# First feed-forward product in pairs of units: 64-row products of two units on the two halves of the array's rows

## The chip, the cores and the metric

The kernel runs on one core of a Trainium2 chip. The metric is the device time of one execution in microseconds. Before the change the median of three runs is 411.9 us (411.26 to 412.43).

## What is computed

The input x has 2048 rows (tokens) of 448 values. With xn the layer norm of x, the output is x, plus a spectral filter of xn, plus a mixer of xn:

```
X = rfft2(xn) * (w_r + 1j * w_i);  A = irfft2(X)              # 2048 x 448
h = gelu(layernorm(xn) @ w1);  hs = shift(h) @ w2;  x1 = xn + hs
B = x1 + gelu(layernorm(x1) @ w3) @ w4                         # w3: 448 x 1792, w4: 1792 x 448
out = x + A + B
```

The change concerns `layernorm(x1) @ w3`, the first product of the feed-forward part.

## The kernel before, in words

All products run in f16 and carry each operand as a high and a low part; a product is the sum of three passes, high by high, high by low and low by high. The 448 rows of w3 are a contraction of three full strips of 128 and a last strip of 64. `w3p` holds high parts in strips 0 to 3 and low parts in strips 4 to 7; strip 3 holds its 64 rows twice, in the lower and the upper half of the partitions, and so does strip 7. The tokens' side `x2all` holds strips 0 to 3 high and 4 to 6 low; in strip 3 the partitions 0 to 63 are the high part of the last 64 values and partitions 64 to 127 their low part. So strip 3 of `w3p` by strip 3 of `x2all` is two passes in one product, and strip 7 by strip 3 is the third pass (`mlp_in`, L425 to L429, the product itself at L427). That makes 3 + 3 + 3 + 2 = 11 products for each block of 128 columns of w3.

The feed-forward work is cut into 56 units: 8 groups G of 256 tokens by 7 pieces fp of 256 columns. `front` (L745) makes a unit's 22 products of 128x256 into one PSUM bank (L427), then ScalarE applies gelu in place (L753) and writes the high part (L756), and VectorE writes the low part (L757) to a tile `hf`, of which there are three. `back` (L761) multiplies `hf` by w4 (L776), 12 products of 448 columns, into the group's two accumulators. `mlp` (L791) calls these in turn: for groups 0 to 2 two units ahead, alternately on the banks tagged "mm" and "tr" (two of each), from group 3 on one unit ahead, on the two "mm" banks.

A scheduler with priorities and a model of time orders the instructions of each engine; the feed-forward work has the lowest priority (FILL), so it fills TensorE between the steps of the other branch. Those are step1 (L594), and then 16 chunks, each with products at L651 (pp), L668 (px) and L697 (pu) and conversions on ScalarE, VectorE and GpSimd (L658 to L701), and at the end the inverse transform (L717, L739). Between the 56 units stand also w_scale_end (L617, L621), which spreads one scale: L621 multiplies a single row. Other products that a step below uses are L254 (a sum over partitions, one column), L406 (the turning of x by an identity, of 128 and of 64 columns) and L456 and L501 (w1 and w2).

`ln2` (L512) writes each block of 128 tokens as `h`, 896 columns: 0 to 447 high, 448 to 511 the low part of the last 64, 512 to 895 the other low parts. SyncE turns it with a DMA transpose into `x2all` (L544). The other transposes on SyncE's queue are those of the w1 result (L483, `h<-hs`) and of x (L833).

Of the kernel before, what the change touches and what calls it, by code (L numbers as in the profile page):

```python
# [13 lines left out]
F16 = mybir.dt.float16  # L14
# [17 lines left out]
AH = 2  # L32
# [89 lines left out]
def body(tc, nc, x, wf, w1, w2, w3, w4, c_g, c_n, c_small, out):  # L122
    V, A, P, T, SY = nc.vector, nc.scalar, nc.gpsimd, nc.tensor, nc.sync
# [28 lines left out]
    def bank(tag, name):  # L152
        return ps.tile([128, 512], F32, tag=tag, bufs=2, name=name)
# [3 lines left out]
    pw = pool("pw")  # L157
# [62 lines left out]
    load_x(3)  # L220
    load_w3([2, 3])
    x2mem = pw.tile([128, 9 * F], F16, name="x2mem")
    x2all = x2mem[:, 0:8 * F].rearrange("p (j t n) -> p j t n", j=4, t=7)
    w4raw = x2mem.bitcast(F32)[:, F:].rearrange("p (f n) -> p f n", f=14)
    W4F = (0, 4, 8, 11, 14)
# [198 lines left out]
    def mlp_in(ps_out, wp, cols, xT, tok, ts=range(4)):  # L424
        for t in ts:  # L425
            for wi, xi in ((0, 0), (0, 4), (4, 0)) if t < 3 else ((0, 0), (4, 0)):
                T.matmul(ps_out, wp[:, wi + t, cols], xT[:, xi + t, tok],  # L427
                         start=t == 0 and wi + xi == 0, stop=t == 3 and wi == 4)


    w3p = pa.tile([128, 8, F], F16, name="w3p")
# [79 lines left out]
    def ln2(bs, engines, pins=None):  # L511

        n, b0 = len(bs), bs[0]
        mv = stats([xb(b) for b in bs], f"b{b0}")
        a = pc.tile([128, 4], F32, tag="vb", bufs=2, name=f"vb{b0}")[:, :n]
        r = pc.tile([128, 4], F32, tag="vs", bufs=2, name=f"vs{b0}")[:, :n]
        o, y = [], []
        nm = pc.tile([128, 4], F32, tag="nm", bufs=2, name=f"nm{b0}")[:, :n]
        P.tensor_scalar(out=nm, in0=mv[:, :n, 0], scalar1=-1.0, scalar2=None, op0=ALU.mult)
        for m in range(0, n, 2):  # L520
            w = stage(f"y{b0 + m}", 8 * 448, 0 if pins else (b0 + m) // 2 % 2, F16)
            o.append(w[:, 0:4 * D].bitcast(F32).rearrange("p (i n) -> p i n", i=2))
# [12 lines left out]
        for i in range(n):  # L535
            b, h, x_ = b0 + i, y[i // 2][:, i % 2], o[i // 2][:, i % 2]
            k = r[:, i:i + 1]
            with behind("f", *pins[i]) if pins else contextlib.nullcontext():
                u = A.activation(out=h[:, 0:D], in_=x_, func=AF.Copy, scale=k)
                V.scalar_tensor_tensor(out=h[:, 448:512], in0=x_[:, 384:448], scalar=k, in1=h[:, 384:448],  # L540
                                       op0=ALU.mult, op1=ALU.subtract)
                v = V.scalar_tensor_tensor(out=h[:, 512:896], in0=x_[:, 0:384], scalar=k, in1=h[:, 0:384],
                                           op0=ALU.mult, op1=ALU.subtract)
            d = SY.dma_start_transpose(out=x2all[:, b // 4][:, :, 128 * (b % 4):128 * (b % 4) + 128], in_=h)  # L544
            after[f"b{b0}"] = u.ins, v.ins, d.ins

    def unscaled(b, t=None):
# [194 lines left out]

    acc, hs, rest = {}, {}, {}

    def front(G, fp, tag):  # L745
        tok = slice(256 * (G % 2), 256 * (G % 2) + 256)
        pm = bank(tag, f"pw3_{G}{fp}")
        for ff in range(2):
            f = 2 * fp + ff
            mlp_in(pm[:, 256 * ff:256 * ff + 256], w3p, slice(128 * f, 128 * f + 128), x2all[:, G // 2], tok)  # L750
        with prio(EVAC):
            with behind("te", 12) if (G, fp) == (4, 1) else contextlib.nullcontext():
                A.activation(out=pm, in_=pm, func=AF.Gelu_apprx_tanh, scale=r3)  # L753
            h = pw.tile([128, 2, 512], F16, tag="hf", bufs=3, name=f"hf{G}{fp}")
            with behind("te", 10 + 2 * fp) if (G, fp) in ((4, 1), (4, 2)) else contextlib.nullcontext():
                i = A.activation(out=h[:, 0], in_=pm, func=AF.Copy, scale=h3)  # L756
                j = V.scalar_tensor_tensor(out=h[:, 1], in0=pm, scalar=h3, in1=h[:, 0], op0=ALU.mult, op1=ALU.subtract)  # L757
            after["f", G, fp] = i.ins, j.ins
        hs[G, fp] = h
# [28 lines left out]
                    V.scalar_tensor_tensor(out=xb(b), in0=acc[G][i][:, :D], scalar=p34[:, 0:1], in1=xb(b),  # L788
                                           op0=ALU.mult, op1=ALU.add)

    def mlp(Gs, last=False, hook=None, ahead=1, tags=("mm",)):  # L791
        with prio(FILL):
            todo = [(G, fp) for G in Gs for fp in range(7)]
            done = 0
            for n, (G, fp) in enumerate(todo):
                while done < min(n + 1 + ahead, len(todo)):
                    front(*todo[done], tags[done % len(tags)])
                    if hook:
                        with prio(EVAC):
                            hook(*todo[done])  # L800
                    done += 1
                if fp == 3 and last:
                    for b in (2 * G, 2 * G + 1):
                        rest[b] = unscaled(b, x2mem.bitcast(F32)[:, D * (b - 12):D * (b - 11)])
                back(G, fp)


    wps = bank("mm", "wps")
# [136 lines left out]
    for k in range(4):  # L945
        n = 128 if k < 3 else 64
# [39 lines left out]
        w4_split(2)  # L986

    def w4_rest(G, fp):
        if fp < 5:
# [21 lines left out]
    mlp([1, 2], ahead=AH, tags=("mm", "tr"))  # L1011
    for b in range(0, NB, 2):
        do_fold(b)
        step1_in(b)
# [22 lines left out]
        if 0 <= i - 3 < NC:  # L1037
            chunk_c(i - 3)
    close("pst")
    mlp(range(3, 6))  # L1040
    pv = pool("pv", side="right")
    bs = [*range(12, 16), *range(8, 12), *range(8)]
    units = [(G, fp) for G in range(4, 8) for fp in range(7)][INV:]
# [9 lines left out]
                finish(bs[n])  # L1053

    inverse(range(4))
    mlp([6], last=True)
    inverse(range(4, 16))
    mlp([7], last=True)
    for name in ("pv", "pa2", "pa", "pw", "px", "pc", "ps"):
        close(name)  # L1060

# [23 lines left out]
```

## Time and profile before

| | |
|---|---|
| median of 3 runs | 411.9 us |
| span of the profiled execution | 409.9 us |
| its own time: the span, and some 2.0 us around it by the median | about 411.9 us |
| granted TensorE clock | 1.000 |
| instructions | 8512 |
| TensorE weight loads (PEld) busy | 288.1 us |
| VectorE busy | 294.8 us |
| ScalarE busy | 247.8 us |
| GpSimd busy | 116.8 us |
| mean DMA traffic | 121 GB/s |

Busy time of TensorE is from the starts of its products to modelled ends, which overlap; what a product costs in a row of products is the distance from start to start. In the listings a row of the timeline is start, length, engine, line, operation, tiles, shapes and count, neighbours of one line merged; a row of the chain is start, length, engine, tile, line and count.

### The profile page before, as it was taken

Reading aid. Unit: us, or ns where it says so; the run is one execution under the profiler, and the core shown is the slowest. Engines: PE = TensorE matmul, PEld = TensorE weight load, DVE = VectorE, ACT = ScalarE, POOL = GpSimd, SP = SyncE. Lnnn points to the kernel's source line nnn. Section 1 sums busy time; section 2 is a strip of 40 time slices with the busy share of each in tenths; the row PEclk is TensorE's granted clock in tenths of the full one; section 3 lists DMA queues with packets and bytes.
Section 4 is the critical chain, followed back from the end, with each engine's and each line's share of the span. In section 5 each row is a group of like instructions: output and inputs, shape, how many; then the busy total and the mean of one; then the engine's idle time right before and its main releaser. Section 6 shows DMA issues by size and latency. Waiting matters only on the chain.

```text
span 409.9 us, 8512 instructions
## 1 busy us (share of the span) xinstructions
PE 404.8 (99%) x3295; PEld 288.1 (70%) x3295; DVE 294.8 (72%) x642; ACT 247.8 (60%) x427; POOL 116.8 (29%) x206
## 2 busy tenths in 40 slices
PE   8999999999999999999999999999999999999996
PEld 4554556666677877776887887877776777677885
DVE  5989999898644658863689889875777787667122
ACT  4689994884738756861688888873343434342321
POOL 3889820002308745400021221111222221121000
PEclk9999999999999999999999999999999999999999
DMA  8999999907712283527056555610000213223001
GB/s 278 335 269 200 172 178 248 269 2 183 137 43 56 79 300 106 143 63 164 14 162 167 145 147 142 182 43 2 2 0 2 73 55 100 91 76 128 24 0 46
DMA packets 57208, 49.45 MB, mean 121 GB/s; under 512 B 41312, under 2 KB 52192, under 8 KB 57168
## 3 DMA queue, kind: packets, MB, share of 16 engines
q1 hardware_dynamic: 57168, 48.91, 45.5%
q8 instruction: 26, 0.43, 0.4%
q14 instruction: 14, 0.11, 0.1%
HBM read 35.06 MB, written 3.67 MB: 95 GB/s over the span
## 4 chain that ended last, share of the span: by engine, by line
PE 96%; DMA 1%; POOL 1%; DVE 1%; issue 0%; POOLq 0%
PE pw L427 33%; PE acc L776 31%; PE pw L501 9%; PE pw L456 6%; PE pu L697 3%; PE ps L594 3%; PE pp L651 2%; PE pe L717 2%; PE px L668 2%; PE py L739 2%; PE wps L812 2%; DMA h<-hs 1%; PE pta L406 1%; POOL w2s L273 0%; POOL w2s L901 0%
## 5 line engine op out<-in xcount | busy, mean ns | idle before, releaser
L427 PE MATMUL pw<-x2mem,w3p 128*128 128x256 f16 x1232 | 149.1, 272 | 0.0
L776 PE MATMUL acc<-w4p,hf 128*128 128x448 f16 (+1 forms) x714 | 138.0, 341 | 0.0
L427 PEld LDWEIGHTS <-w3p 128*128 128x128 f16 x1232 | 118.6, 98 | 19.0
L776 PEld LDWEIGHTS <-hf 128*128 128x128 f16 x714 | 69.4, 98 | 48.3 <-DVE hf L757 0.3
L753 ACT ACTIVATE pw<-pw,pe 128x512 f32<-128x512 f32 x56 | 36.7, 655 | 63.1 <-PE pw L427 62.0
L757 DVE SCALAR_TENSOR_TENSOR hf<-pw,h,hf 128x512 f16<-128x512 f32 x56 | 42.0, 749 | 44.7 <-ACT hf L756 44.3
L756 ACT ACTIVATE hf<-pw,h 128x512 f16<-128x512 f32 x56 | 38.3, 684 | 1.2
L501 PE MATMUL pw<-w2p,h 112*128 112x448 f16 x192 | 38.8, 352 | 0.1
L678 POOL TENSOR_TENSOR z<-te 128x450 f32<-128x450 f32 x16 | 16.0, 1001 | 72.9 <-DVE te L676 69.1
L456 PE MATMUL pw<-w1p,xT 128*128 128x448 f16 x176 | 34.9, 352 | 0.5 <-DVE h L875 0.5
L724 POOL TENSOR_TENSOR e<-e 128x226 f32<-128x226 f32 x16 | 11.5, 720 | 77.8 <-ACT e L721 74.6
L501 PEld LDWEIGHTS <-h 112*128 112x128 f16 x192 | 18.5, 98 | 16.9 <-DMA h<-hs 0.9
L456 PEld LDWEIGHTS <-xT 128*128 128x128 f16 x176 | 17.0, 98 | 16.4 <-ACT xT L416 0.7
L658 ACT ACTIVATE pf<-pp 64x450 f16<-64x450 f32 x32 | 17.3, 541 | 16.7 <-DVE pf L659 8.3
L721 ACT ACTIVATE e<-pe 128x452 f32<-128x452 f32 x16 | 8.8, 547 | 26.4 <-PE pe L717 26.4
L659 DVE TENSOR_TENSOR pf<-pp,pf 64x450 f16<-64x450 f32 x32 | 19.9, 621 | 5.8 <-ACT pf L658 5.6
L574 POOL TENSOR_TENSOR xr<-xf 128x452 f32<-128x452 f32 x8 | 8.9, 1109 | 35.9 <-issue 27.1
L673 ACT ACTIVATE te<-px 64x450 f32<-64x450 f32 x32 | 17.2, 537 | 0.5
L585 DVE TENSOR_TENSOR xh<-f,xh 128x452 f16<-128x452 f32 x16 | 13.4, 878 | 5.3 <-ACT xh L584 5.3
L732 DVE TENSOR_TENSOR vh<-e,vh 128x448 f16<-128x448 f32 x16 | 10.0, 624 | 9.7 <-ACT vh L731 9.7
L577 POOL TENSOR_TENSOR f<-xr 128x452 f32<-128x452 f32 x16 | 16.4, 1045 | 0.6
L726 DVE TENSOR_TENSOR e<-e 128x113 f32<-128x113 f32 x16 | 9.9, 619 | 7.8 <-POOL e L724 7.8
(171 smaller groups left out, 598.8 us busy)
## 6 DMA issues: line engine op xcount, KB each, us to landing
wc<-wf SPq DMA_DIRECT2D x32, 225.0 KB, 3.5
wl<-wf SPq DMA_DIRECT2D x8, 450.0 KB, 4.1
xf<-x SPq DMA_DIRECT2D x8, 448.0 KB, 3.5
xt<-x SPq DMA_DIRECT2D x3, 896.0 KB, 12.1
w3raw<-w SPq DMA_DIRECT2D x3, 896.0 KB, 15.3
xr<-x SPq DMA_DIRECT2D x12, 224.0 KB, 2.6
out<-xr SPq DMA_DIRECT2D x12, 224.0 KB, 2.0
gn<-c_g SPq DMA_DIRECT2D x16, 128.0 KB, 3.2
```

The costliest lines, as they stand in the source:

```text
L427: T.matmul(ps_out, wp[:, wi + t, cols], xT[:, xi + t, tok], start=t == 0 and wi + xi == 0, stop=t == 3 and wi == 4)
L456: m = T.matmul(pm[:, :D], xTs[g][:, xi + t, 128 * i:128 * i + 128], w1p[:, wi + t], start=t == 0 and p == 0, stop=t == 3 and p == 2)
L501: m = T.matmul(w2b[b][:, :D], hT[g][:112, 4 * hi + k, o:o + 128], w2p[:, wi, k], start=k == 2 and hi + wi == 0, stop=k == 3 and hi == 1)
L577: P.tensor_tensor(out=f[:, :, k:k + 2].rearrange("p b s d -> p s b d"), in0=u[:, :, 0], in1=u[:, :, 1], op=op)
L658: A.activation(out=hi, in_=src, func=AF.Copy)
L659: V.tensor_tensor(out=lo, in0=src, in1=hi, op=ALU.subtract)
L673: i = A.activation(out=e[64 * h:64 * h + 64], in_=px_[64 - 64 * h:128 - 64 * h, :2 * DF], func=AF.Copy)
L678: P.tensor_tensor(out=z, in0=t[:, 0], in1=t[:, 1], op=ALU.add)
L753: A.activation(out=pm, in_=pm, func=AF.Gelu_apprx_tanh, scale=r3)
L756: i = A.activation(out=h[:, 0], in_=pm, func=AF.Copy, scale=h3)
L757: j = V.scalar_tensor_tensor(out=h[:, 1], in0=pm, scalar=h3, in1=h[:, 0], op0=ALU.mult, op1=ALU.subtract)
L776: m = T.matmul(to, h[:, hi, o:o + 128], w4p[0][:, wi, f, r], start=f == 0 and n == 0, stop=f == 13 and n == 2)
```

## The change

The strip-7 product contracts 64 rows only: the high part of the last 64 values by the low part of w3. Units are made in pairs. The first unit's 64-row products take `w3p[0:64]` with `x2all[0:64]`; the second unit's take `w3p[64:128]` with a new tile `x2d`, whose partitions 64 to 127 hold the same high part, written by a second DMA transpose of columns 320 to 447 of `h`. Each unit first makes its other 20 products; then the pair's four 64-row products follow, first unit, second unit, first unit, second unit. `hf` gets a fourth buffer, `mlp` runs over all 56 units with one count and calls pairs ahead, on the two "mm" or the two "tr" banks in turn for pairs that begin in groups 0 to 2 and on the two "mm" banks for the others. The scratch space for software-made DMA descriptors is made smaller.

```diff
+    x2d = pw.tile([128, 4, 512], F16, name="x2d")
...
             d = SY.dma_start_transpose(out=x2all[:, b // 4][:, :, 128 * (b % 4):128 * (b % 4) + 128], in_=h)
+            SY.dma_start_transpose(out=x2d[:, b // 4, 128 * (b % 4):128 * (b % 4) + 128], in_=h[:, 320:448])
...
-    def front(G, fp, tag):
+    def half(pm, ff, f, G, r, stop):
         tok = slice(256 * (G % 2), 256 * (G % 2) + 256)
-        pm = bank(tag, f"pw3_{G}{fp}")
+        x = x2d[64:128, G // 2, tok] if r else x2all[0:64, G // 2, 3, tok]
+        T.matmul(pm[:, 256 * ff:256 * ff + 256], w3p[64 * r:64 * r + 64, 7, 128 * f:128 * f + 128], x, start=False, stop=stop)
+
+    def fronts(units, tag):
+        pms = []
+        for G, fp in units:
+            tok = slice(256 * (G % 2), 256 * (G % 2) + 256)
+            pm = bank(tag, f"pw3_{G}{fp}")
+            for ff in range(2):
+                f = 2 * fp + ff
+                for t in range(4):
+                    for wi, xi in ((0, 0), (0, 4), (4, 0)) if t < 3 else ((0, 0),):
+                        T.matmul(pm[:, 256 * ff:256 * ff + 256], w3p[:, wi + t, 128 * f:128 * f + 128],
+                                 x2all[:, G // 2, xi + t, tok], start=ff + t + wi + xi == 0, stop=False)
+            pms.append(pm)
         for ff in range(2):
-            f = 2 * fp + ff
-            mlp_in(pm[:, 256 * ff:256 * ff + 256], w3p, slice(128 * f, 128 * f + 128), x2all[:, G // 2], tok)
+            for r, (G, fp) in enumerate(units):
+                half(pms[r], ff, 2 * fp + ff, G, r, ff == 1)
+        for (G, fp), pm in zip(units, pms):
+            halves(G, fp, pm)
+
+    def halves(G, fp, pm):
...
-            h = pw.tile([128, 2, 512], F16, tag="hf", bufs=3, name=f"hf{G}{fp}")
+            h = pw.tile([128, 2, 512], F16, tag="hf", bufs=4, name=f"hf{G}{fp}")
...
-    def mlp(Gs, last=False, hook=None, ahead=1, tags=("mm",)):
+    todo = [(G, fp) for G in range(8) for fp in range(7)]
+    done = [0, 0]
+
+    def mlp(last, hook=None):
         with prio(FILL):
...
+            while done[1] < 7 * last + 7:
+                G, fp = todo[done[1]]
+                while done[0] < min(done[1] + 4 - done[1] % 2, len(todo)):
+                    units = todo[done[0]:done[0] + 2]
+                    fronts(units, ("mm", "tr")[done[0] // 2 % 2] if units[0][0] < 3 else "mm")
...
+                    done[0] += 2
...
                 back(G, fp)
+                done[1] += 1
...
-    mlp([0], hook=w4_rest, ahead=AH, tags=("mm", "tr"))
+    mlp(0, w4_rest)
...
-    nc = bacc.Bacc("TRN2", target_bir_lowering=False, num_devices=1)
+    nc = bacc.Bacc("TRN2", target_bir_lowering=False, num_devices=1, dynamic_dma_scratch_size=512)
```

More of the change, by code (lines that the diff above doesn't have):

```diff
@@ L789, in back @@
                                            op0=ALU.mult, op1=ALU.add)
-    def mlp(Gs, last=False, hook=None, ahead=1, tags=("mm",)):
+    todo = [(G, fp) for G in range(8) for fp in range(7)]
+    done = [0, 0]
+    def mlp(last, hook=None):
         with prio(FILL):
[L793 to L797, printed above, removed]
+            while done[1] < 7 * last + 7:
[3 more added lines that the diff above has]
+                    fronts(units, ("mm", "tr")[done[0] // 2 % 2] if units[0][0] < 3 else "mm")
                     if hook:
                         with prio(EVAC):
-                            hook(*todo[done])
-                    done += 1
-                if fp == 3 and last:
+                            for u in units:
+                                hook(*u)
+                    done[0] += 2
+                if fp == 3 and G > 5:
                     for b in (2 * G, 2 * G + 1):
@@ L988, in w4_rest @@
     def w4_rest(G, fp):
-        if fp < 5:
+        if G == 0 and fp < 5:
             with behind("f", G, fp):
                 w4_split(2 * fp + 4)
-    mlp([0], hook=w4_rest, ahead=AH, tags=("mm", "tr"))
+    mlp(0, w4_rest)
     ln2(range(4, 8), [P, A, P, A])
@@ L1010, in body @@
         P.memset(xh_buf[i][:, 904:], 0.0)
-    mlp([1, 2], ahead=AH, tags=("mm", "tr"))
+    mlp(2)
     for b in range(0, NB, 2):
@@ L1039, in body @@
     close("pst")
-    mlp(range(3, 6))
+    mlp(5)
     pv = pool("pv", side="right")
@@ L1055, in body @@
     inverse(range(4))
-    mlp([6], last=True)
+    mlp(6)
     inverse(range(4, 16))
-    mlp([7], last=True)
+    mlp(7)
     for name in ("pv", "pa2", "pa", "pw", "px", "pc", "ps"):
```

## The prediction, made before the changed kernel ran

> **What bounds the kernel now.** I read the page first: busy shares, the chain that ended last, and the costliest groups.
>
> ```profile
> span 409.9 us, 8512 instructions
> PE 404.8 (99%) x3295; PEld 288.1 (70%) x3295; DVE 294.8 (72%) x642; ACT 247.8 (60%) x427; POOL 116.8 (29%) x206
> ...
> PE 96%; DMA 1%; POOL 1%; DVE 1%; issue 0%; POOLq 0%
> ...
> L427 PE MATMUL pw<-x2mem,w3p 128*128 128x256 f16 x1232 | 149.1, 272 | 0.0
> L776 PE MATMUL acc<-w4p,hf 128*128 128x448 f16 (+1 forms) x714 | 138.0, 341 | 0.0
> ...
> L753 ACT ACTIVATE pw<-pw,pe 128x512 f32<-128x512 f32 x56 | 36.7, 655 | 63.1 <-PE pw L427 62.0
> L757 DVE SCALAR_TENSOR_TENSOR hf<-pw,h,hf 128x512 f16<-128x512 f32 x56 | 42.0, 749 | 44.7 <-ACT hf L756 44.3
> L756 ACT ACTIVATE hf<-pw,h 128x512 f16<-128x512 f32 x56 | 38.3, 684 | 1.2
> ```
>
> TensorE is the bound: 96% of the chain, and no idle time ahead of the two large groups, L427 (the product that the change splits) and L776. The next view is the chain in order of time, a stretch of the inverse stage, to see what one product costs in a row of products.
>
> ```profile
> 341.16 2.40 PE pw L427 x22
> 343.56 2.27 PE acc L776 x12
> 345.84 0.57 PE py L739 x3
> 346.40 0.61 PE pe L717 x12
> 347.02 2.40 PE pw L427 x22
> ```
>
> Each piece begins where the one before ends. A unit's 22 products take 2.40 us, so 109 ns each, far below the 272 ns that the page gives as the length of one; the rest of the 272 is time in the pipeline, which overlaps with the next product. So 109 ns is what a removed product is worth, and any wait put between products is added to the end one for one.
>
> **What the change takes away.** A pair of units has four strip-7 products, 4 x 109 = 436 ns. Afterwards they are four 64-row products, and in the built program the first unit's stand on rows 0 to 63 of the array and the second's on rows 64 to 127. If two on different halves run beside each other, the four take 2 x 109 = 218 ns, and a lag of the second behind the first. There are 28 pairs, at most 28 x 218 ns = 6.1 us. The order of the built program says how many get it: 25 pairs have their four products in one run; one pair, (4,0) with (4,1), has two runs of one product of each unit with chunk work between; two pairs, (4,2) with (4,3) and (4,4) with (4,5), are pulled apart by the scheduler into four runs of two products of the same unit, which share their rows and can't overlap. That is 31 runs, each with an entry from full-height products and an exit back to them.
>
> **What the change of height costs.** The trace of before has one place where TensorE goes from 128 rows to fewer and back: L621, one row, in a strip of 32 rows by the built program. I read it in the timeline with narrow windows, so that single products show.
>
> ```profile
> 194.65 0.27 PE L427 MATMUL pw<-x2mem,w3p 128*128 128x256 f16 x1
> 194.85 0.38 PE L621 MATMUL wpb<-wt,ones 1*128 1x1 f32 x2
> ```
>
> ```profile
> 194.99 0.24 PE L621 MATMUL wpb<-wt,ones 1*128 1x1 f32 x1
> 195.16 0.22 PE L651 MATMUL pp<-csm,y 113*128 113x113 f16 x1
> ```
>
> ```profile
> 194.85 0.29 PEld L621 LDWEIGHTS wpb<-wt,ones 1*128 1x128 f32 x2 [0.21 <-issue]
> ```
>
> The last L427 starts at 194.65 and L621 at 194.85: 200 ns, where L427 is otherwise followed after 109. Its weight load does not start under the running product (in the page's shares loads lie beside products nearly always: 404.8 and 288.1 of 409.9 us), but after 0.21 us idle, and what ended that wait is "issue", no semaphore. So the entry costs 200 - 109 = 90 ns. This predecessor is the very product that stands ahead of the runs of the change. For the exit I need the same tiny f32 product at full height, which is L254:
>
> ```profile
> 20.57 0.28 PE L254 MATMUL pm<-pt,ones 128*128 128x1 f32 x2
> 20.71 0.54 PE L456 MATMUL pw<-w1p,xT 128*128 128x448 f16 x2
> ```
>
> ```profile
> 20.60 0.25 PE L254 MATMUL pm<-pt,ones 128*128 128x1 f32 x1
> ```
>
> From the second L254 to the f16 product behind it are 20.71 - 20.60 = 110 ns, from the second L621 195.16 - 194.99 = 170: the exit costs 60 ns behind a product of one column. The whole visit (two products) lasts 195.16 - 194.85 = 310 ns against 20.71 - 20.57 = 140 for L254, so with the entry it costs 90 + 170 = 260; part of that is the slow f32 load that is no longer hidden. How long an f16 load shows after the switch, and how close two products may follow, the neighbours tell:
>
> ```profile
> 195.16 0.10 PEld L651 LDWEIGHTS <-y 113*128 113x128 f16 x1
> ```
>
> ```profile
> 195.18 0.15 PEld L651 LDWEIGHTS <-y 113*128 113x128 f16 x2
> ```
>
> ```profile
> 195.78 0.49 PE L427 MATMUL pw<-x2mem,w3p 128*128 128x256 f16 x3
> ```
>
> ```profile
> 197.31 0.77 PE L651 MATMUL pp<-csm,y 113*128 113x113 f16 x12
> 197.91 0.28 PE L427 MATMUL pw<-x2mem,w3p 128*128 128x256 f16 x1
> ```
>
> The 12 products behind the switch take 195.78 - 195.16 = 620 ns and the same 12 a chunk later 600, so an open f16 load costs 0 to 20 ns, I take 10. The second load follows the first after 20 ns; I take that as the lag of the second half, with 0 and the 50 ns of one L651 (600 / 12) as its ends.
>
> One run, then: entry 90, exit 90 (taken from the entry, since a 256-column product stands ahead of it as there, not from the exit's 60), open loads 20, together 200 ns.
> - 25 full runs: 200 + 218 + 20 = 438 ns against 436, +0.05 us in all.
> - 4 runs of one unit: 218 as before and 200 more each, +0.8 us.
> - 2 runs of the split pair: 200 + 109 + 20 = 329 against 218, +0.2 us.
>
> Sum: +1.1 us. The lower end (90 + 60, no load, no lag) gives 25 x -68 ns, 4 x 150 and 2 x 41, so -1.0 us; the upper end (260 for each visit, lag 50) 25 x 92, 4 x 260 and 2 x 201, so +3.7 us.
>
> The Trainium skill speaks against the change in the same way: TensorEngine Tiling (Array Packing), section Key Properties, says "Mode switching requires drain", a change of tiling mode and not of the tile alone. By that rule, the trace agrees for rows (90 ns at L621); the page counts 128x64 among the modes too, and there the trace differs (rival 1). It gives no price, and the sum by it stays where it is.
>
> **What else moves.** SyncE gets 16 more transposes.
>
> ```profile
> L544 SPq DMA_TRANSPOSE x2mem<-y x16: 1221/1274/2798, 56.9 to 185.1; - x16
> ```
>
> At most 16 x 1.27 = 20 us of SyncE's time. In the new order one stands among the h transposes of group 2, the others where SyncE waits anyway or where nothing near is due. I take 0; the upper end is one of them on the chain, 1.3 us. The fourth hf buffer takes a wait away that the groups above don't show; 0. The smaller descriptor scratch matters to no queue here, as the page's section on queues has all the data on the hardware queue; 0:
>
> ```profile
> q1 hardware_dynamic: 57168, 48.91, 45.5%
> ```
>
> Pairs make the work coarser: from group 3 on, two fronts take both "mm" banks. The next pair needs the first bank after two backs, 2 x 2.27 = 4.54 us; emptying it takes 0.655 + 0.684 + 0.749 = 2.1 us, and the second bank is needed 20 x 109 ns = 2.2 us later still, when ScalarE and VectorE have had 6.7 us for 2 x 1.34 + 0.75 = 3.4. That holds where they are free. In the chunk stage VectorE is nearly full (columns: PE, PEld, DVE, ACT, POOL busy):
>
> ```profile
> 220.00:230.00 10.00, 10.00 (x116) 8.53 (x114) 9.35 (x16) 8.51 (x16) 1.97 (x2) 1.00 0.66 164
> 250.00:260.00 10.00, 10.00 (x107) 8.20 (x106) 9.57 (x16) 7.92 (x16) 2.29 (x3) 1.00 0.55 146
> ```
>
> It has 0.4 to 0.7 us free in 10 us, TensorE none, so TensorE waits wherever the new order asks for chunk steps faster. In the new order px12 and px13 stand closer together than before. I take 0.5 us for all such stalls; from 0 (the order is made for it) to 2.0 (with the transposes). The sum is +1.1 + 0.5 = +1.6 us on the profiled execution, whose span of 409.9 and the 2.0 around it are the median, 411.9: **413.5 us**, its own range 410.9 (-1.0) to 417.6 (+5.7).
>
> **Rivals.**
> 1. No wait at the change of height (faster). The wait at L621 may belong to the one-row f32 product, not to a strip of rows. For this speaks L406, where TensorE goes from 128 columns to 64 and back:
>
> ```profile
> 21.47 1.04 PE L406 MATMUL pta<-ident,xt 128*128 128x128 f32 x8
> 22.34 8.65 PE L456 MATMUL pw<-w1p,xT 128*128 128x448 f16 x44
> ```
>
> ```profile
> L406 PE MATMUL pta<-ident,xt 128*64 128x128 f32 x4 | 0.6, 272 | 0.0
> ```
>
> Four of these eight have 64 columns, and the eight take (22.34 - 21.47) / 8 = 109 ns each: a narrower product costs no wait on either side. Against it: those keep all rows, and L254, f32 and one column too, has no such wait. Then 25 x (218 - 20) ns and 2 x (109 - 20) are gained, 5.1 us, and with TensorE that much faster VectorE's reserve in the chunks gives perhaps 0.8 back: 407.6 us, from 406.2 with no lag and no stall. It decides from the point where entry, exit and loads cost less than 5.1 us / 31 = 165 ns a run.
>
> The Trainium skill has a figure for the lag: TensorE: Matmul & The Clock Gate, section Measured speedup vs the span model, gives about 4 ns for each further tile and 3.07 times for four row tiles. By it the 25 full runs would gain 16 ns more each, 0.4 us; no run here shows it.
>
> 2. The halves don't overlap (it doesn't do what it says). Nothing in the trace shows two products beside each other: the closest f16 products, those of L651, start 50 ns apart. Then the 64-row products cost 109 each as before, and the 31 runs 200 ns each come on top: +6.2, and 0.5 of stalls, 418.6 us. Without waits at the change of height as well it would be 412.4.
>
> 3. Stalls in the chunk stage grow: if VectorE must be waited for at each of the four chunks 12 to 15 by the 0.5 us that I took for all, 2.0 us in place of 0.5, 415.0 us. This is inside my own range and its upper half rests on it.
>
> **How the numbers follow.** A measurement of this kernel tells about 0.3% (1.2 us) from no change. Wait and overlap (forecast): 0.70; its own range reaches from 410.9 to 417.6, with 0.02 faster, 0.22 within 0.3% and 0.46 slower, since its middle lies 0.4 us beyond the bound. No wait, overlap: 0.20, all faster. Wait, no overlap: 0.07, slower. Neither: 0.03, within 0.3%. So faster 0.22, same 0.25, slower 0.53. The range leaves out the rival at 418.6 (0.07), the top of my own range (0.06) and the lowest part of the first rival (0.05): 407.0 to 416.2. The likeliest case's own range is 410.9 to 417.6.
>
> **What would show it.** In the timeline of the changed kernel, at a run of 64-row products: the first starts some 200 ns after the last full product (109 if rival 1 holds), the second within 50 ns of the first (109 if rival 2 holds), and the full product behind them some 200 ns after the fourth. In the waits, PEld would show idle time put down to "issue" at both ends of a run, some 60 times. Stalls would show as idle time of TensorE on ScalarE or VectorE between 200 and 285 us. The prediction is wrong if the entry is at 109 ns, if the exit costs far more or less than the entry, or if TensorE waits for a bank or a transpose for more than 2 us in all.

## The result and the profile after

The changed kernel takes 417.8 us (median of 4 runs, 416.99 to 418.36) beside 412.1 for the kernel before (median of 4, 411.26 to 412.43): ratio 1.0143, 95% interval 1.0126 to 1.016. It is 5.7 us slower; a slower kernel was forecast, but the time is 4.3 us above the 413.5 and 1.6 us above the top of the range (416.2), 0.2 above that of the likeliest case (417.6). The profiled execution has a span of 415.9 us, beside 409.9.

The page after, first busy shares and chain, then the two large groups of TensorE, and the w2 products:

```profile
span 415.9 us, 8544 instructions
PE 406.6 (98%) x3295; PEld 278.0 (67%) x3295; DVE 291.6 (70%) x642; ACT 243.5 (59%) x427; POOL 117.2 (28%) x206
...
PE 93%; DMA 3%; ACT 2%; DVE 1%; issue 0%; SPq 0%; ACTq 0%
...
L796 PE MATMUL acc<-w4p,hf 128*128 128x448 f16 (+1 forms) x714 | 137.4, 342 | 0.8 <-ACT hf L776 0.8
L761 PE MATMUL pw<-x2mem,w3p 128*128 128x256 f16 x1120 | 131.6, 272 | 0.0
...
L502 PE MATMUL pw<-w2p,h 112*128 112x448 f16 x192 | 38.9, 352 | 2.3 <-DMA h<-hs 1.9
```

TensorE has as many products as before and is still the bound. But its part of the chain fell from 96 to 93%, and two groups now have idle time ahead of them that had next to none (0.0 and 0.1 us): L796 (L776 before) waits for ScalarE, and L502 (L501 before) for a transpose. Neither is a 64-row product (L750).

The chain in the inverse stage, where nothing but the products themselves can count:

```profile
343.79 4.37 PE pw L761 x40
348.16 0.33 PE pw L750 x4
348.49 2.38 PE acc L796 x12
```

A pair's 40 products take 4.37 us, 109 ns each as before. Four 64-row products in 0.33 us and a w4 group that takes 2.38 in place of 2.27 (the chain counts the wait ahead of its first product as part of it): 0.44 us for what four full products did in 0.436. A single run in narrow windows of the timeline shows why:

```profile
124.46 0.27 PE L761 MATMUL pw<-x2mem,w3p 128*128 128x256 f16 x1
124.67 0.28 PE L750 MATMUL pw<-x2mem,w3p 64*128 64x256 f16 x1
124.67 0.28 PE L750 MATMUL pw<-x2d,w3p 64*128 64x256 f16 x1
124.79 0.27 PE L750 MATMUL pw<-x2mem,w3p 64*128 64x256 f16 x1
124.79 0.27 PE L750 MATMUL pw<-x2d,w3p 64*128 64x256 f16 x1
```

```profile
124.99 0.36 PE L796 MATMUL acc<-w4p,hf 128*128 128x448 f16 x1
```

The two halves of a row of products stand on the same hundredth of a microsecond: they run beside each other. The first comes 0.21 us after the last full product (the entry), and the full product behind the run 0.20 us after the last half (the exit), where 0.11 is usual. From full product to full product the run lasts 124.99 - 124.46 = 0.53 us, against 5 x 109 = 545 ns before. By the trace's stamps in ns, the 25 whole runs have an entry of 205 (the first one stands behind L502, a longer product, and has 285 in place of 189: 96 more, as the others), a lag of 3 to 4 between the halves, 115 to 117 to the second two, and an exit of 201 to 202, 529 or 530 in all. So a whole run gains 15 ns, 0.4 us for 25; the four runs of one unit last 526 or 527 against 327 (+0.8), the two short ones, one product of each unit, 0.19 more together: **+0.6 us** for what the change does itself. The weight loads' waits, from the waits of the weight loader (total, times, longest), show the same two ends:

```profile
PEld L750 <- issue: 6.5, 30, 0.4
PEld L796 <- issue: 5.3, 25, 0.2
```

The other 5 us come from elsewhere. Busy time by windows, before and then after (length, then PE, PEld, DVE, ACT, POOL, the granted clock, DMA):

```profile
60.00:95.00 35.00, 35.00 (x219) 21.13 (x218) 32.38 (x90) 23.21 (x39) 2.65 (x10) 1.00 0.63 165
255.00:285.00 30.00, 30.00 (x285) 23.49 (x284) 21.50 (x41) 19.78 (x35) 5.03 (x6) 1.00 0.29 79
```

```profile
60.00:95.00 35.00, 32.43 (x202) 19.05 (x201) 27.98 (x82) 20.87 (x35) 2.41 (x5) 1.00 0.74 177
255.00:285.00 30.00, 28.21 (x269) 20.66 (x268) 23.90 (x39) 22.48 (x40) 6.14 (x6) 1.00 0.40 102
```

TensorE was full in both before; now it is idle for 2.57 and 1.79 us, and the time lost is somewhat more, since the modelled end of an L761 lies some 160 ns behind the start of the next (272 - 109). The granted clock is 1.00 in all four rows.

**Place one, near 65 us.** The chain after, and the SyncE rows of the timeline, before and then after:

```profile
64.61 7.11 DMA h<-hs
```

```profile
59.57 1.06 SPq L228 DMA_DIRECT2D x2mem<-w  x2
65.05 6.68 SPq L483 DMA_TRANSPOSE h<-hs  x4
```

```profile
60.68 1.22 SPq L546 DMA_TRANSPOSE x2d<-y  x1
61.95 1.05 SPq L229 DMA_DIRECT2D x2mem<-w  x2
64.61 9.83 SPq L484 DMA_TRANSPOSE h<-hs  x4
```

Two new x2d transposes stand ahead of the first load of w4 (`x2mem<-w`), this one and one at 49.96. The load is issued 2.4 us later than before, while the h transposes come a little earlier. The four of them now keep SyncE's queue for 9.83 us in place of 6.68, waits between them included, and the chain runs through one that takes 7.11 us to land. Why it lands late, the stamps of the landings show: before, the second of the two loads lands at 67.95 and the first h transpose, issued at 65.05, at 69.01; after, the load at 70.73 and the first h transpose, issued at 64.61, at 71.72. Both times it lands 1.0 to 1.1 us behind the load, and in none of the traces of this document does a transfer on SyncE's queue land ahead of one that was issued before it. So a load that starts later makes the transposes behind it land later, although they were issued no later. How small the new transpose is does not help SyncE; the rows of the two lines (min/median/max, ns):

```profile
L545 SPq DMA_TRANSPOSE x2mem<-y x16: 1233/1249/1831, 58.0 to 188.7; - x16
```

```profile
L546 SPq DMA_TRANSPOSE x2d<-y x16: 1093/1204/1767, 50.0 to 190.0; - x16
```

x2d's has 128 columns, the other 896, and they cost the queue 1.20 and 1.25 us.

**Place two, near 265 us.** The chain after:

```profile
261.61 0.58 ACT zb L687
...
262.83 0.54 ACT te L675
...
263.93 0.55 ACT pw L773
...
265.04 0.58 ACT hf L776
...
265.66 0.93 PE acc L796 x4
```

From 261.6 to 265.7 the chain is a row of ScalarE's instructions without a gap. At L796 TensorE waits for the `hf` of unit (4,1), and ScalarE makes that `hf` (L773, L776) behind two steps of chunk 12 (te L675). The waits of TensorE between 255 and 285 us, the two largest rows:

```profile
PE acc L796 <- ACT hf L776: 0.8, 2, 0.6
PE pu L699 <- PE px L670: 0.5, 1, 0.5
```

So the direct waits for `hf` are 0.8 us of it (for (4,1) and (4,2)); the other 1.0 are waits ahead of the chunks' own products (L699 and L670). That these hang on the holds too, experiment 8 shows, where all of them are gone. ScalarE comes so late because `halves` says so: the gelu of unit (4,1) is held `behind("te", 12)`, and the `hf` of (4,1) and (4,2) `behind("te", 10 + 2 * fp)`. In the kernel before the same lines stood in `front`. They are an order of issue on ScalarE and VectorE, written for single units; a pair brings unit (4,1) to TensorE earlier among the chunks: before, its last product starts at 254.33 and its gelu at 257.42; after, at 247.37 and 263.83.

My theory, then: the 64-row runs themselves are worth little more than nothing, and the loss is (a) the x2d transposes, by way of the w4 load beside the h transposes, and (b) the holds, by way of the pair order. The rivals: the runs cost more than their stamps say, the transposes cost SyncE as such, or the pairs stall whatever the holds. The kernel before was measured anew beside each group of experiments, and its medians differ by 0.5 us, so kernels are compared by their ratios to it. Percentages are of its time; 0.1% is 0.4 us.

### The profile page after: what moved, and what is told of

It reads as the page before. It is cut to its first block, busy times and chain, and to the rows that moved or that the text cites. A ratio compares the mean times of both kernels' runs of the same rounds, so it can differ in the third digit from the quotient of the medians.

```text
span 415.9 us, 8544 instructions
## 1 busy us (share of the span) xinstructions
PE 406.6 (98%) x3295; PEld 278.0 (67%) x3295; DVE 291.6 (70%) x642; ACT 243.5 (59%) x427; POOL 117.2 (28%) x206
## 4 chain that ended last, share of the span: by engine, by line
PE 93%; DMA 3%; ACT 2%; DVE 1%; issue 0%; SPq 0%; ACTq 0%
PE acc L796 31%; PE pw L761 28%; PE pw L457 8%; PE pw L502 6%; PE ps L596 3%; PE pw L750 2%; PE pe L719 2%; PE pu L699 2%; PE py L741 2%; PE pp L653 2%; PE px L670 2%; PE wps L837 2%; DMA h<-hs 2%; DMA x2mem<-w 1%; PE pta L407 1%; ACT xr L243 1%
## 5 line engine op out<-in xcount | busy, mean ns | idle before, releaser
L796 PE MATMUL acc<-w4p,hf 128*128 128x448 f16 (+1 forms) x714 | 137.4, 342 | 0.8 <-ACT hf L776 0.8
L761 PE MATMUL pw<-x2mem,w3p 128*128 128x256 f16 x1120 | 131.6, 272 | 0.0
L761 PEld LDWEIGHTS <-w3p 128*128 128x128 f16 x1120 | 108.5, 98 | 16.5 <-issue 0.2
L796 PEld LDWEIGHTS <-hf 128*128 128x128 f16 x714 | 66.3, 98 | 54.9 <-issue 5.3
L777 DVE SCALAR_TENSOR_TENSOR hf<-pw,h,hf 128x512 f16<-128x512 f32 x56 | 40.5, 745 | 44.4 <-ACT hf L776 44.3
L773 ACT ACTIVATE pw<-pw,pe 128x512 f32<-128x512 f32 x56 | 34.8, 654 | 43.3 <-PE pw L750 43.2
L502 PE MATMUL pw<-w2p,h 112*128 112x448 f16 x192 | 38.9, 352 | 2.3 <-DMA h<-hs 1.9
L776 ACT ACTIVATE hf<-pw,h 128x512 f16<-128x512 f32 x56 | 36.6, 689 | 0.2
L733 ACT ACTIVATE vh<-e 128x448 f16<-128x448 f32 x16 | 9.2, 577 | 39.7 <-DVE e L731 39.7
L502 PEld LDWEIGHTS <-h 112*128 112x128 f16 x192 | 18.5, 98 | 19.1 <-DMA h<-hs 2.4
L675 ACT ACTIVATE te<-px 64x450 f32<-64x450 f32 x32 | 17.3, 539 | 4.5 <-PE px L670 4.0
L587 DVE TENSOR_TENSOR xh<-f,xh 128x452 f16<-128x452 f32 x16 | 10.9, 725 | 11.0 <-ACT xh L586 11.0
L676 DVE SCALAR_TENSOR_TENSOR te<-px,sc,wc 128x450 f32<-128x450 f32 x16 | 11.0, 685 | 5.9 <-ACT te L675 5.4
L808 DVE SCALAR_TENSOR_TENSOR xt<-acc,p,xt 128x448 f32<-128x448 f32 x12 | 8.1, 679 | 9.8 <-PE acc L796 9.8
```

What stands on the lines that cost most here:

```text
L502: m = T.matmul(w2b[b][:, :D], hT[g][:112, 4 * hi + k, o:o + 128], w2p[:, wi, k], start=k == 2 and hi + wi == 0, stop=k == 3 and hi == 1)
L675: i = A.activation(out=e[64 * h:64 * h + 64], in_=px_[64 - 64 * h:128 - 64 * h, :2 * DF], func=AF.Copy)
L761: T.matmul(pm[:, 256 * ff:256 * ff + 256], w3p[:, wi + t, 128 * f:128 * f + 128], x2all[:, G // 2, xi + t, tok], start=ff + t + wi + xi == ...
L796: m = T.matmul(to, h[:, hi, o:o + 128], w4p[0][:, wi, f, r], start=f == 0 and n == 0, stop=f == 13 and n == 2)
```

## The experiments

**1. The runs alone** (`e1_full_height`). Strip 7 at full height, all else as after, the instructions in the same order.

```diff
-        x = x2d[64:128, G // 2, tok] if r else x2all[0:64, G // 2, 3, tok]
-        T.matmul(pm[:, 256 * ff:256 * ff + 256], w3p[64 * r:64 * r + 64, 7, 128 * f:128 * f + 128], x, start=False, stop=stop)
+        T.matmul(pm[:, 256 * ff:256 * ff + 256], w3p[:, 7, 128 * f:128 * f + 128], x2all[:, G // 2, 3, tok], start=False, stop=stop)
```

> The changed kernel with the strip-7 products back at full height (all 128 rows of w3p strip 7 by x2all strip 3, for both units); pairs, order of every engine and the 16 extra transposes stay. Theory: the 31 visits to half height cost little in sum (trace of the changed kernel: 25 full runs 530 ns from product to product against 5 x 109 = 545, four runs of one unit 526 against 327, two short ones 94 too long, +0.6 us in all), and the rest of the loss, some 5 us, is waits elsewhere. Then this kernel takes 417.8 - 0.6 = 417.2 us, 416.7 to 417.6. Rival: the changes of height are the cause of the loss, also of the waits; then about 412.

Measured 417.5 us, ratio 1.0124 (1.0103 to 1.0145). So nearly all of the loss stays when no product has 64 rows. The difference to after is 0.3 us by the medians and 0.19% or 0.8 us by the ratios, within the intervals; it agrees with the +0.6 us of the stamps and doesn't prove it. That strip 7 at full height does not bring the time back means that the waits near 65 and 265 us don't come from the change of height.

**2. Whether the halves overlap** (`e2_same_rows`). Both units' 64-row products on rows 0 to 63.

```diff
-        x = x2d[64:128, G // 2, tok] if r else x2all[0:64, G // 2, 3, tok]
-        T.matmul(pm[:, 256 * ff:256 * ff + 256], w3p[64 * r:64 * r + 64, 7, 128 * f:128 * f + 128], x, start=False, stop=stop)
+        T.matmul(pm[:, 256 * ff:256 * ff + 256], w3p[0:64, 7, 128 * f:128 * f + 128], x2all[0:64, G // 2, 3, tok], start=False, stop=stop)
```

> The changed kernel with both units' 64-row products on rows 0 to 63 (w3p[0:64] by x2all[0:64]), everything else and the order as they are. Theory: two products on different halves run beside each other and two on the same half do not; each full run grows by 2 x 109 - 14 = 204 ns, 25 of them 5.1 us, the two short ones 0.2 more: 423.1 us, 422 to 423.5. Rival: the overlap seen in the trace is only in the recorded starts and brings nothing; then 417.8.

Measured 424.0 us, ratio 1.0284 (1.0256 to 1.0312), 0.5 us above the expected range. In the timeline, two windows (L760 and L749 are the lines L761 and L750 of the changed kernel):

```profile
126.89 0.27 PE L760 MATMUL pw<-x2mem,w3p 128*128 128x256 f16 x1
127.09 0.28 PE L749 MATMUL pw<-x2mem,w3p 64*128 64x256 f16 x1
```

```profile
127.09 0.39 PE L749 MATMUL pw<-x2mem,w3p 64*128 64x256 f16 x2
```

The second product now starts about 0.11 us behind the first (the two of them are 0.39 long, one is 0.28; by the stamps 119 or 120 ns, and 109 or 110 for the third and fourth). Whole runs last 745 ns in place of 530, 25 x 215 = 5.4 us, most of the 6 us or so between this kernel and after. The entry is again 0.20: the wait belongs to the change of height and not to two halves at work. Nor does every smaller height have it: in the trace of before a product of 112 or 113 rows (L501, L717) comes the usual 109 ns behind an L427.

**3. The transposes in the kernel before** (`e3_before_transposes`). They are added and nobody reads them.

```diff
+    x2d = pw.tile([128, 4, 512], F16, name="x2d")
...
+            SY.dma_start_transpose(out=x2d[:, b // 4, 128 * (b % 4):128 * (b % 4) + 128], in_=h[:, 320:448])
...
-    nc = bacc.Bacc("TRN2", target_bir_lowering=False, num_devices=1)
+    nc = bacc.Bacc("TRN2", target_bir_lowering=False, num_devices=1, dynamic_dma_scratch_size=512)
```

> The kernel before with the 16 extra transposes into a tile that nothing reads; no pairs, no half height. Theory: the first two of them push the load of w4 on SyncE's queue some 2.4 us later, into the transposes of the last w1 group, which then land late, and TensorE waits for them: about 3 us more, 415 us, 414 to 416. Rival: SyncE has room for them and the wait at the start comes from the pairs; then 412.

Measured 414.3 us, ratio 1.0057 (1.0035 to 1.0078): +2.3 us from transposes that no product waits for, a little under what was expected. The SyncE rows are those of after:

```profile
61.99 1.05 SPq L229 DMA_DIRECT2D x2mem<-w  x2
64.46 9.70 SPq L484 DMA_TRANSPOSE h<-hs  x4
```

**4. No transposes** (`e5_copies`). GpSimd copies the high part from `x2all` in four pieces.

```diff
-            SY.dma_start_transpose(out=x2d[:, b // 4, 128 * (b % 4):128 * (b % 4) + 128], in_=h[:, 320:448])
+            if b % 4 == 3:
+                P.tensor_copy(out=x2d[64:128, b // 4], in_=x2all[0:64, b // 4, 3])
```

> The changed kernel with x2d filled by four copies on GpSimd (each 64x512, from x2all's partitions 0 to 63 to x2d's 64 to 127) in place of the 16 transposes. Theory: SyncE's queue is then as before the change, the waits near the start (2.1 us at the w2 products, 0.5 and 0.4 behind) go, those between 260 and 280 us stay: 414.8 us, 414.2 to 415.4. Rival: the waits near the start come from the order of the pairs; then above 416.5.

Measured 415.3 us, ratio 1.0081 (1.0068 to 1.0094): 0.62% less than after, 2.6 us, near what was expected.

**5. The first two transposes later** (`e4_transposes_late`). They stand behind the other w4 loads; `x2d_turn` issues the line that is taken out.

```diff
-            SY.dma_start_transpose(out=x2d[:, b // 4, 128 * (b % 4):128 * (b % 4) + 128], in_=h[:, 320:448])
+            if b > 1:
+                x2d_turn(b, h)
+            else:
+                held.append((b, h))
...
+        for b, h in held:
+            x2d_turn(b, h)
```

> The changed kernel with the first two extra transposes issued behind the second load of w4 in place of ahead of the first; the other 14 stay. Theory: the wait of about 3 us near the start goes, the waits between 260 and 280 us stay: 414.8 us, 414 to 415.5. Rival: the extra transposes cost whatever their place, or the wait comes from the order of the pairs; then 417.8.

Measured 416.5 us, ratio 1.0103 (1.0075 to 1.0132): a miss by 1.7. The wait near 69 us has shrunk from 1.9 to 0.4 us, but others came; the longest, in the waits of TensorE:

```profile
PE pw L758 <- DMA x2d<-y: 0.7, 1, 0.7
```

The second unit's first 64-row product (L758 here) now waits for the transpose that was put off. By this run alone it stays open whether it is the transposes or what they push that is slow.

**6. The w4 load away from the h transposes** (`e11_w4_late`). The x2d transposes stay; all four w4 loads come behind the last group of h transposes.

```diff
-    with behind("t", 3), behind("h", 2, 3), behind("b0"):
-        for i in range(2):
-            load_w4(i)
...
-        for i in range(2, 4):
+        for i in range(4):
             load_w4(i)
```

> The changed kernel with all four loads of w4 behind the last group of h transposes. If the first w4 load is what the h transposes collide with, the transposes of that group take about 1.3 us each to issue and land in about 3.3 us, and TensorE's wait of 2.1 us at the w2 products near 69 us goes. The scale of w4 then comes later, which may cost 1 to 3 us at the first products with w4: 415 to 418 us in all, against 417.8. Rival: the transposes are slow by themselves, since x2d's stand between them; then the wait at the w2 products stays at 1.5 us or more.

Measured 414.6 us, ratio 1.0079 (1.0064 to 1.0094): 0.64% less than after, 2.6 us. SyncE's rows and TensorE's window:

```profile
60.40 1.23 SPq L546 DMA_TRANSPOSE x2d<-y  x1
64.40 5.94 SPq L484 DMA_TRANSPOSE h<-hs  x4
70.40 2.28 SPq L229 DMA_DIRECT2D x2mem<-w  x4
```

```profile
60.00:95.00 35.00, 35.00 (x228) 21.37 (x227) 30.64 (x90) 21.58 (x37) 2.44 (x9) 1.00 0.71 179
```

The same four h transposes take 5.94 us, and TensorE does not wait at all between 60 and 95 us, with the x2d transpose where it was. That is the decisive one for place one: the load ahead of the h transposes costs, not SyncE's 1.2 us. The 1 to 3 us that I had allowed for the later scale of w4 did not appear, so the time is below the expected 415 to 418.

**7. The pair order alone** (`e6_pair_order`). Strip 7 at full height, no x2d and no second transpose; with the holds.

```diff
-    x2d = pw.tile([128, 4, 512], F16, name="x2d")
...
-            SY.dma_start_transpose(out=x2d[:, b // 4, 128 * (b % 4):128 * (b % 4) + 128], in_=h[:, 320:448])
...
-        x = x2d[64:128, G // 2, tok] if r else x2all[0:64, G // 2, 3, tok]
-        T.matmul(pm[:, 256 * ff:256 * ff + 256], w3p[64 * r:64 * r + 64, 7, 128 * f:128 * f + 128], x, start=False, stop=stop)
+        T.matmul(pm[:, 256 * ff:256 * ff + 256], w3p[:, 7, 128 * f:128 * f + 128], x2all[:, G // 2, 3, tok], start=False, stop=stop)
```

> The order of pairs alone: strip-7 products at full height, no x2d, no extra transposes. Theory: only the waits between 260 and 280 us are left of the loss, 2.5 us on the kernel before: 414.5 us, 414 to 415. Rival: the pairs as such cost nothing and the waits there come from the visits to half height; then 412.

Measured 413.9 us, ratio 1.0054 (1.0039 to 1.0068): +2.2 us from the order, just under the expected range. Its window has the idle time of after, with no transposes and no 64-row product in the kernel:

```profile
255.00:285.00 30.00, 28.14 (x273) 21.74 (x272) 23.13 (x43) 21.26 (x38) 5.17 (x5) 1.00 0.36 93
```

**8. The changed kernel without the holds** (`e7_no_holds`).

```diff
-            with behind("te", 12) if (G, fp) == (4, 1) else contextlib.nullcontext():
-                A.activation(out=pm, in_=pm, func=AF.Gelu_apprx_tanh, scale=r3)
+            A.activation(out=pm, in_=pm, func=AF.Gelu_apprx_tanh, scale=r3)
...
-            with behind("te", 10 + 2 * fp) if (G, fp) in ((4, 1), (4, 2)) else contextlib.nullcontext():
+            with contextlib.nullcontext():
```

> The changed kernel without the two holds in halves, which keep gelu and copies of units (4,1) and (4,2) behind the te steps of chunks 12 and 14. Theory: the waits between 260 and 280 us come from these holds: pairs reach these units earlier against the chunks, ScalarE then holds their banks, and TensorE is left with chunk steps too close together (px12 to px13 is 2.4 us of products in the changed order, 5.5 without holds, while ScalarE and VectorE need some 4 us for a chunk). Without them 417.8 - 2.7 = 415.1 us, 414.5 to 416. Rival: two fronts in a row on two banks are the cause, holds or not; then 417 or more.

Measured 414.3 us, ratio 1.006 (1.0047 to 1.0073): 0.83% less than after, 3.4 us, somewhat more than expected. Part of it is not the stall: without the holds the four runs of one unit are gone too. This trace has 26 whole runs and four short ones, and by the stamps the whole ones gain 0.4 us and the short ones lose as much, where the runs of the changed kernel lost 0.6; so some 2.8 us are left for the stall. TensorE is full at place two:

```profile
255.00:285.00 30.00, 30.00 (x302) 23.40 (x300) 23.44 (x38) 21.00 (x38) 5.89 (x6) 1.00 0.41 103
```

**9. The kernel before without the holds** (`e10_before_no_holds`), the control: the same edit in `front`.

> The kernel before without the two holds on the units of group 4. If the holds only hurt where pairs bring those units forward, this is the time before, 412.0 us within 0.5, with no new idle time of TensorE between 255 and 285 us. Rival: the holds cost the kernel before something as well, and taking them away gives 1 us or more there too, 411.0 or less; then the gain of taking them out of the changed kernel is not due to the pairs.

Measured 412.4 us, ratio 1.0016 (1.0005 to 1.0027). There the holds are worth a little (0.16%); only with pairs do they cost.

**10. Both mended** (`e8_copies_no_holds`: the edits of 4 and 8; `e12_late_no_holds`: the edits of 6 and 8, with all the 16 transposes).

> Both together: copies on GpSimd and no holds. If the three causes (16 transposes, holds, 31 visits to half height) add up, what is left on the kernel before is the price of the visits, with all 28 pairs in whole runs: 28 x (530 - 545) = -0.4 us, so 411.5 to 412.5 us. Rival: pairs cost something else; then above 413.

> The changed kernel with its 16 second transposes, all four w4 loads behind the last group of h transposes, and no holds. If the two stalls are all of the cause, the gains of the single edits add up: 417.8 - 3.5 for the holds - 3.2 for the w4 loads = 411.1 us, from 410.8 to 411.8, the same as the kernel before within 0.2%, with no idle time of TensorE over 0.5 us between 60 and 100 us and between 255 and 285 us. Rival: the transposes cost SyncE time on the path elsewhere as well, up to 1.3 us of it; then 412.3 or more.

Measured 412.0 us, ratio 1.0006 (0.9997 to 1.0015), and 411.6 us, ratio 0.9998 (0.9988 to 1.0007). The single gains add up: 0.83 + 0.64 = 1.47% by runs 8 and 6, and 1.43 + 0.02 = 1.45% for both at once. Both kernels came out within the expected ranges. In the second kernel, with its transposes, pairs and 64-row runs:

```profile
60.00:95.00 35.00, 35.00 (x228) 21.43 (x227) 30.89 (x90) 21.85 (x37) 2.65 (x9) 1.00 0.71 180
255.00:285.00 30.00, 30.00 (x294) 23.24 (x292) 21.38 (x34) 20.28 (x37) 4.90 (x5) 1.00 0.40 102
```

Both places are full. The rival that the transposes cost SyncE elsewhere (412.3 or more) falls. The 64-row runs, 26 of them whole there and two pairs pulled apart into four short runs, leave the time of the kernel before within 0.1%, as they should: 26 x 15 ns are gained and 4 x 93 lost.

**11. Fewer visits** (`e9_quads`, `e13_later_quads`). Groups of four units on four banks with eight buffers of `hf`, so that eight 64-row products share one entry and one exit: on top of `e8_copies_no_holds` for units 0 to 19, and on top of `e12_late_no_holds` for units 8 to 19. The main lines of the first edit:

```diff
-                half(pms[r], ff, 2 * fp + ff, G, r, ff == 1)
+                half(pms[r], ff, 2 * fp + ff, G, r % 2, ff == 1)
...
-            h = pw.tile([128, 2, 512], F16, tag="hf", bufs=4, name=f"hf{G}{fp}")
+            h = pw.tile([128, 2, 512], F16, tag="hf", bufs=8, name=f"hf{G}{fp}")
...
-                while done[0] < min(done[1] + 4 - done[1] % 2, len(todo)):
-                    units = todo[done[0]:done[0] + 2]
+                while done[0] < min(done[1] - done[1] % 4 + 8 if done[0] < 20 else done[1] + 4 - done[1] % 2, len(todo)):
+                    units = todo[done[0]:done[0] + (4 if done[0] < 20 else 2)]
```

> The changed kernel with both stalls mended as in the two experiments before (copies by GpSimd in place of the second transposes, no holds on the units of group 4), and with groups of four units instead of two for the first 20 units: their eight 64-row products stand in one run. If a run costs two waits of about 95 ns and one row of half products per pair of rows, a run of eight lasts 205 + 3 x 113 + 4 + 202 = 750 ns from the last full product to the next full one, in place of 9 x 109 = 981: 0.23 us less for each, some 0.9 us less than the kernel before over four whole groups, so about 411.0 us, 410.4 to 411.6, with the pairs that remain worth 15 ns each. Rival: four banks filled in a burst and emptied one after the other make TensorE wait for ScalarE and VectorE; then 412 or more, with idle time of TensorE on hf or on the banks before 150 us.

> The kernel of the run before with groups of four units for units 8 to 19 only, behind the first units, where the kernel of quads had waited for ScalarE. Each whole run of eight 64-row products lasted 748 ns there from the last full product to the next, in place of 981: three of them give 0.7 us, less the 2 x 15 ns each that their pairs gave: 0.6 us less than the run before, if no wait comes with them. Rival: the burst of four units makes TensorE wait for hf or delays the steps of the other branch, as in the kernel of quads; then slower than the run before by 1 us or more.

Measured 422.3 us, ratio 1.0268 (1.0252 to 1.0285), and 412.4 us, ratio 1.0018 (1.0009 to 1.0026). The gain of the run itself is there: in the later kernel the eight products from 141.52 on

```profile
141.52 0.28 PE L750 MATMUL pw<-x2mem,w3p 64*128 64x256 f16 x1
...
141.86 0.27 PE L750 MATMUL pw<-x2d,w3p 64*128 64x256 f16 x1
142.06 0.74 PE L795 MATMUL acc<-w4p,hf 128*128 128x448 f16 x3
```

bring the next full product 0.54 us after the first of them, 748 ns after the last full one by the stamps, in place of 981. But other waits come. TensorE's in the first kernel, and ScalarE's there between 88 and 100 us:

```profile
PE acc L796 <- ACT hf L776: 6.5, 1, 6.5
PE ps L597 <- DVE y L602: 2.0, 4, 0.9
```

```profile
ACT y L530 <- DMA x2mem<-y: 7.6, 2, 7.0
```

The gelus of the first four units stand on ScalarE behind a step of `ln2` (L530) that waits 7.0 us for a transpose. The 6.5 us of idle time cost more than themselves: the granted clock behind them is lower. Between 90 and 105 us it is 0.77 in the mean (the third figure from the end), where the kernel before has 1.00, and the four L796 in it take 574 ns each by the profile in place of 352.

```profile
90.00:105.00 15.00, 8.51 (x52) 5.09 (x50) 11.86 (x35) 10.52 (x17) 2.51 (x8) 0.77 0.62 153
```

With the groups of four behind that place, as in the second kernel, this wait is gone; smaller ones stay in the other branch, on VectorE (0.7 us ahead of L699, 0.6 ahead of L596).

Only two of the three groups of the second kernel stay whole, the third is taken apart by the scheduler: about 2 x 0.2 us are gained (748 - 109 = 639 against 2 x 421 ns) and more lost. So in both runs the rival's side came true, in the second at 0.8 us where it had said 1 or more. No version here beats the kernel before by more than the measurement tells.

## Why the prediction was wrong, step by step

- **TensorE is the bound, 109 ns a product:** right as far as the runs tell. The 25 x 215 ns more of run 2 came out as some 6 us, and the versions without idle time of TensorE at both places (run 10) have the time of before.
- **Which runs there are:** right, 25 whole, four of one unit, two short ones in the trace.
- **"entry 90, exit 90":** right; 205 - 109 = 96 and 202 - 109 = 93. The exit is that of the entry's 256-column product, as chosen, and not the 60 of L621.
- **The lag of the second half:** mis-sized, 20 ns taken, 3 to 4 measured. The figure that the prediction cites from the Trainium skill for the lag, TensorE: Matmul & The Clock Gate, section Measured speedup vs the span model, about 4 ns, was the better one: the trace agrees. With the open loads (20 taken, some 10 seen: 119 in place of 109 from the first half to the third) the sum of this part was +1.1 us and came out at +0.6; run 1 is in keeping with it.
- **"At most 16 x 1.27 = 20 us of SyncE's time ... I take 0; the upper end is one of them on the chain, 1.3 us":** this step failed. They cost 2.3 us (run 3) to 2.6 us (runs 4 and 6). The count of SyncE's time was right and the question was wrong: not which transpose is itself on the chain, but which transfer the queue issues behind it, and what has to wait for that one. "The others where SyncE waits anyway or where nothing near is due" overlooked the w4 load directly behind one of them, and the h transposes that land only behind that load.
- **"I take 0.5 us for all such stalls; from 0 ... to 2.0 (with the transposes)":** failed as well. The place was seen ("px12 and px13 stand closer together than before"), the cause was not: VectorE's reserve was priced, and what came late was ScalarE's work in its order of issue, fixed by the holds of units (4,1) and (4,2). It cost 2.2 us (run 7) to some 2.8 us (run 8, without its share of the runs). With place one the stalls come to some 5 us where 0.5 was taken.
- **Slower:** came true, but for another reason than forecast. Of the +1.6 us the runs were to give 1.1; they give 0.6, which is less than a measurement tells from no change, and the stalls priced at 0.5 give the rest. That the direction was right is in good part luck.
- **`hf` buffers and descriptor scratch at 0:** not tried one by one; both are in run 10's second kernel, which ends at the time of before.
- **Rival 1** (no wait at the change of height) falls by the entry of 205 ns, **rival 2** (no overlap) by run 2. **Rival 3**, stalls in the chunks, named the right stage and nearly the price, 2.0 us against the 2.2 of run 7, but not the cause: VectorE, not the holds. It left place one out.
- Its argument from L406 for rival 1, and its remark on 128x64, are not borne out: these products of 64 columns are transposes by an identity, no row tells in which mode of the array they run, and no run here changed the columns.
- The last sentence on what would make it wrong, waits "for a bank or a transpose for more than 2 us in all", is nearly what happened: TensorE idles 2.3 us ahead of L502, 1.9 of them put down to the transpose, and 0.8 ahead of L796 for `hf`.

Open: that the transposes land only behind the load is what the stamps show; what makes it so, was not tried, only that parting the two ends it. Of the pieces added to the kernel before, 2.3 (run 3), 2.2 (run 7) and 0.6 us make 5.1 of 5.7; taken out of the changed kernel they make it whole (run 10). The small remainder is not assigned to one of them.

## What to carry to other kernels

A short DMA on a full queue is priced by what it pushes: list the transfers issued behind it, and see which of them then stand ahead of one that the bound engine is about to need. Hand-written order (a unit held behind a step) is tuned to one order of units; whoever changes the order should take the holds out first and see. Two half-height products on the two halves of the array do cost one, but a change to 64 rows and back costs some 190 ns, so at 109 ns a product a run of four gains next to nothing (15 ns) and needs more of them before it pays, and the units that must be gathered for it have to be emptied somewhere.

## What the runs showed of the hardware

- Products on rows 0 to 63 and 64 to 127 start 3 to 4 ns apart and cost the time of one; on the same rows they follow after 109 to 120 (run 2).
- Going from 128 rows to 64 costs TensorE 96 ns, and going back 93 behind four or eight products, or two on the same rows (exits of 201 to 202 ns). Behind a single product, or one of each half, the exit is 211 to 213. It is the same where all 64-row products share their rows.
- Products of 112 and 113 rows behind one of 128 have no such wait: 109 ns behind an L427 in the trace of before.
- A DMA transpose of 128 columns keeps SyncE's queue for 1.20 us, one of 896 columns for 1.25 (medians of 16).
- Transfers on SyncE's queue land in the order of their issue in all 15 traces. Four h transposes behind a w4 load issued 2.7 us ahead kept the queue for 9.83 us, behind one issued 5.5 us ahead (before) for 6.68, and with the load behind them for 5.94.
- Behind 6.5 us without a product the granted clock was 0.77 over 15 us (the first kernel of run 11).
